# Softmax sums turned by one VectorE transposition, decay sums made by a VectorE scan, and a selector for the first units

## The chip, the cores and the metric

One core of one Trainium2 chip runs the whole program in one launch. The metric is the device time of one execution in microseconds (us), as the median of several runs. The profile comes from one further execution of the same program.

## The reference

A decay attention is followed by two feed-forward layers without biases.

```
q, k, v: (4, 8, 576, 64)   f: (4, 8, 576)
log_f  = log(clip(f, 1e-4, 1));  cum = cumsum(log_f, axis=-1)
scores = q @ k.T / 8 + cum[:, :, :, None] - cum[:, :, None, :]      (causal: -1e9 above the diagonal)
attn   = exp(scores - max); attn = attn / (sum(attn) + 1e-9); x = (attn @ v)   -> (2304, 512)
h = x @ w1_in (512 x 2048);  g = h * sigmoid(1.702 h);   y = g @ w1_out (2048 x 512)
h = y @ w2_in (512 x 2048);  g = max(h, 0) + alpha * min(h, 0);  out = g @ w2_out (2048 x 512)
```

All arrays are float32. In a row of scores the term `cum[i]` is the same for every column and drops out of the softmax; the kernel adds only `-cum[j]`.

## The kernel before, in words

A float32 product is made of three fast products: every operand is split into a rounded high part and the remainder (`hi`, `lo`), and `hi*hi + hi*lo + lo*hi` is accumulated in PSUM.

The attention works on units. A unit is a pair of heads of one batch, 16 units in all, and its 576 query rows are two chunks: rows 0 to 255 and rows 256 to 575. Batch 0 does the first chunks of its four units, then their second chunks; the other batches take a unit's two chunks one after the other. `chunk` (L869 on) makes a chunk's scores: for each tile of 128 query rows, the three split products on 64 rows of the array for each of the two heads, and a fourth product whose stationary operand is a matrix of ones and whose moving operand holds the decays `-8 cum[j]` (L884; L878 for the last 64 rows of both heads). VectorE takes the score tile out of PSUM, adds the causal mask and finds the row minimum of the negated scores (L897); ScalarE does the exponential and the row sums (L906). The four or five columns of sums in `ms` become inverses in `rc` (L920, L922, L925). Four transpositions of 32x32 blocks turn them into rows `rt` (L929), one DMA of GpSimd's queue writes the rows to a scratch in DRAM (`rscr`, L932), and two or four DMAs of that queue read them back, spread over 64 partitions, as `RR` (L935). `chunk2`, one chunk behind, transposes the exponentials on TensorE (L969), copies them to `eT` (L518 on ScalarE, L520 on VectorE), multiplies them by v (L983), and VectorE multiplies the result by `RR` into the ring `xr` (L996).

Where a first chunk of batch 0 needs keys and queries, TensorE transposes loaded tiles (`load_pe`, L770) and ScalarE and VectorE write the halves (L518, L523). Other batches are loaded in another layout and transposed by VectorE.

The decays are made at the start. `f` is loaded, clipped (L620) and its logarithm taken (L621). TensorE transposes it (L634), VectorE copies it (L639), and matmuls with a triangle of ones sum it (L648), first for columns 0 to 255, then for the other 320. ScalarE scales by -8 (L657), VectorE splits into halves (L658, L659), and DMAs write them to `cscr` in DRAM (L662, L663). The operand of the fourth product, `dk`, lies in one row for each head and half. For the first chunks of batch 0, four DMAs copy these rows out of `xr` into `w` (L1202; two of SyncE's queue, two of ScalarE's); all others are read from `cscr` into `KB` (L804).

While the attention runs, the first layer's matmuls over finished blocks of `xr` are laid between its instructions on TensorE (`gemm1`, L1027); their weights come through `wraw` (L686). After it come a tail of 768 tokens and the other products (L1050, L1271, L1453), with TensorE as good as always busy.

The order on each engine is written by a planner (`Plan.plan`), a list scheduler with a duration for each operation, and a number of buffers for each pool. Operations with a priority between 1000 and 2000, `gemm1` among them, are held back by the third number of `TRIES` when they compete with others. `Plan.run` also puts in matmuls with no use (fillers, L488) where the planner sees TensorE idle near the start. Each engine and each DMA queue runs its instructions in the order that the planner wrote, so that a waiting one holds all behind it.

Of the kernel before, what the change touches and what calls it, by code (L numbers as in the profile page):

```python
# [7 lines left out]
F32 = mybir.dt.float32  # L8
# [22 lines left out]
TRIES = [(800.0, 3000.0, 800.0)]  # L31
# [218 lines left out]
def kernel(  # L250
# [13 lines left out]
    nc = tc.nc  # L264
# [34 lines left out]
    EB, ET, QS = 2, 6, 2  # L299
# [77 lines left out]
    p_d0 = sl("w", F32R, [1, SPLIT], (1, 8192, NP))  # L377
# [14 lines left out]
    ones = att.tile([P, 2, P], F32R, name="ones")  # L392
    p_z = sb("att", "Z", 2, [P, 2, 2, 64], F32R)
# [16 lines left out]
    p_rt = sb("att", "rt", 3, [P, P])  # L410
# [204 lines left out]
    set_rows("dk0", p_d0, range(NP), lambda: part_of["w", 1][:, 2048:2048 + NP * SPLIT], NP * SPLIT, -85, (), 0, 64)  # L615
# [7 lines left out]
    plan.add([("ACT", 1300.0)], lambda e: nc.scalar.activation(warm, warm, AF.Exp), [b_f, b_id], (), -79)  # L623
    b_ch = Buf()
    chi = lambda: xr[0:BH, 3, RING - S:].bitcast(F32R)
    b_lt = Buf(ps_h)
    for part, (lo, hi) in enumerate(((0, SPLIT), (SPLIT, S))):
        ts_ = [t for t in range(NKT) if lo <= t * P < hi]
        pri = -80 if part == 0 else A0 + P1PRI

        def lf_tr(e, ts_=ts_):
            for t in ts_:
                w = min(P, S - t * P)
                nc.tensor.transpose(b_lt.ap[:w, t * BH:(t + 1) * BH], f_sb()[:, t * P:t * P + w], ident[:BH, :BH])  # L634

        def lf_cp(e, ts_=ts_):
            for t in ts_:
                w = min(P, S - t * P)
                nc.vector.tensor_copy(lfT()[:w, t], b_lt.ap[:w, t * BH:(t + 1) * BH])  # L639

        bb = Buf(ps_v)

        def cum_mm(e, lo=lo, hi=hi, bb=bb):
            tt = [t for t in range(NKT) if t * P < hi]
            for t in tt:
                w = min(P, S - t * P)
                a = max(lo, t * P)
                nc.tensor.matmul(  # L648
                    bb.ap[:BH, a - lo:hi - lo], lfT()[:w, t, :], tri()[:w, a - t * P:hi - t * P],
                    start=(t == 0), stop=(t == tt[-1]),  # L650
                )

        cs = slice(lo, hi)
        plan.add([("PE", 90.0 * len(ts_))], lf_tr, [b_f, b_id], [(b_lt, part)], pri, pad=None if part else (b_lt, lambda: b_lt.ap[:, :P], 0))
        plan.add([("DVE", 100.0 * len(ts_))], lf_cp, [(b_lt, part)], [(b_cl, part)], pri)
        plan.add([("PE", 1350.0 if part == 0 else 3300.0)], cum_mm, [(b_cl, i) for i in range(part + 1)] + [b_tri], [bb], pri, pad=(bb, lambda bb=bb: bb.ap[:, :P], 0))
        plan.add([("ACT", c_act(hi - lo, True))], lambda e, cs=cs, bb=bb, n=hi - lo: nc.scalar.mul(cums()[:, cs], bb.ap[:BH, :n], -8.0), [bb], [(b_cs, part)], pri)  # L657
        plan.add([("DVE", c_dve(hi - lo, True))], lambda e, cs=cs: nc.vector.tensor_copy(chi()[:, cs], cums()[:, cs]), [(b_cs, part)], [(b_ch, part)], pri)  # L658
        plan.add([("DVE", c_dve(hi - lo))], lambda e, cs=cs: nc.vector.tensor_tensor(  # L659
            cuml()[:, cs], cums()[:, cs], chi()[:, cs].bitcast(F32), op=ALU.subtract  # L660
        ), [(b_cs, part), (b_ch, part)], [(b_cc, part)], pri)
        plan.add(DMA(128 * (hi - lo)), lambda e, cs=cs: nc.sync.dma_start(cscr[:, 0, cs], chi()[:, cs].bitcast(F32)), [(b_ch, part)], [(b_cum, (part, 0))], A0 + P1PRI)  # L662
# [179 lines left out]
    def chunk(u, q0, q1, pri):  # L842
# [8 lines left out]
        for j, (t, a, w) in enumerate(tiles):  # L851
# [14 lines left out]
            for c0 in range(0, ext, step):  # L866
# [5 lines left out]
                def mm(e, pms=pms, a=a, w=w, c0=c0, c1=c1, f0=f0):  # L872
# [7 lines left out]
                    for i, (x, y) in enumerate(((qh, kh), (qh, kl), (ql, kh), (None, dk))):  # L880
                        for hh in range(2):
                            r = slice(64 * hh, 64 * hh + 64)
                            l = ones[r, 0, :w] if x is None else x.ap[r, a - qo:a - qo + w]
                            nc.tensor.matmul(pms[hh].ap[:, f0:f0 + c1 - c0], l, y.ap[r, c0:c1], start=i == 0, stop=i == 3, skip_group_check=True)  # L884
# [640 lines left out]
```

## Time and profile before

| | us |
|---|---|
| median of 3 runs | 962.19 (961.74 to 962.71) |
| the profiled execution, its own time | 961.95 |
| its span | 960.2 |
| TensorE busy | 942.9 (98%) |
| VectorE busy | 736.1 (77%) |
| ScalarE busy | 544.1 (57%) |
| GpSimd busy | 71.1 (7%) |

The span runs from the first to the last instruction of the program; some 1.7 us of the execution's time lie around it. PE is TensorE's matmuls, PEld its weight loads, DVE VectorE, ACT ScalarE, POOL GpSimd, SPq SyncE's queue of DMA issues. A busy share is an average over the whole span: the first 250 us hold the attention and half of the first layer, where VectorE is nearly always busy too; after that VectorE and ScalarE have room.

### The profile page before, as it was taken

The numbers are of one execution on the slowest core, as the hardware profiler recorded it, in microseconds if no ns is written. First come the engines' busy times: TensorE is split into PE (matmuls) and PEld (weight loads), VectorE is DVE, ScalarE is ACT, GpSimd is POOL, SyncE is SP. The second block draws the span as 40 slices with busy tenths as digits, with TensorE's granted clock in tenths as the row PEclk, the third lists the DMA queues.
The fourth block names the chain that finished last, engine by engine and source line by source line (L and its number), as shares of the span: only waits on it lengthen the run. The fifth ranks groups of instructions, "written<-read, shape, count | busy, mean of one in ns | idle before, by whom it ended". The sixth has DMA issues, their size and how long they took to land.

```text
span 960.2 us, 18275 instructions
## 1 busy us (share of the span) xinstructions
PE 942.9 (98%) x6499; PEld 870.4 (91%) x6499; DVE 736.1 (77%) x1760; ACT 544.1 (57%) x1197; POOL 71.1 (7%) x149
## 2 busy tenths in 40 slices
PE   8999999999999999999999999999999999999998
PEld 6788787888999999888888988999999999999998
DVE  5899998996167766736758885988568978898987
ACT  6898876676344355657767774566465623221212
POOL 2321233331020000000000000000000000000000
PEclk9999999999999999999999999999999999999999
DMA  7978777542222375548796785688729495443523
GB/s 149 184 187 225 180 135 161 114 86 73 79 72 85 106 249 182 167 156 316 276 321 220 245 270 171 222 322 280 273 90 345 156 395 170 144 151 109 154 78 100
DMA packets 183132, 177.59 MB, mean 185 GB/s; under 512 B 100736, under 2 KB 156832, under 8 KB 180736
## 3 DMA queue, kind: packets, MB, share of 16 engines
q1 hardware_dynamic: 178928, 171.61, 58.1%
q0 software_dynamic: 4096, 4.80, 2.0%
q8 instruction: 51, 0.84, 0.4%
q14 instruction: 41, 0.34, 0.1%
q10 hardware_dynamic: 16, 0.01, 0.0%
HBM read 112.43 MB, written 63.92 MB: 184 GB/s over the span
## 4 chain that ended last, share of the span: by engine, by line
PE 81%; DVE 7%; DMA 4%; issue 3%; ACT 2%; SPq 1%; POOL 1%; DVEq 0%; ACTq 0%; POOLq 0%
PE bk L1050 23%; PE bk L1271 21%; PE bk L1453 19%; PE bk L1027 11%; PE bk L983 3%; PE bk L969 2%; PE bk L884 2%; DMA KB<-cscr 1%; DMA rscr<-rt 1%; PE bk L878 1%; DVE rt L929 1%; DMA RR<-rscr 1%; DVE ec L897 1%; POOL RR L935 1%; DVE ea L897 1%
## 5 line engine op out<-in xcount | busy, mean ns | idle before, releaser
L1050 PE MATMUL bk<-x,wS 128*128 128x384 f32 x912 | 160.7, 335 | 0.9 <-DVE lx L1076 0.9
L1050 PEld LDWEIGHTS bk<-x,wS 128*128 128x128 f32 x912 | 158.1, 188 | 2.0 <-DVE lx L1076 1.8
L1027 PE MATMUL bk<-xh,w 128*128 128x320 f32 (+2 forms) x640 | 148.8, 308 | 0.1
L1271 PE MATMUL bk<-lh,w 128*128 128x512 f32 (+1 forms) x640 | 147.0, 368 | 1.3 <-ACT lh L518 1.3
L1271 PEld LDWEIGHTS bk<-lh,w 128*128 128x128 f32 x640 | 112.8, 189 | 21.6 <-ACT lh L518 1.6
L1027 PEld LDWEIGHTS bk<-xh,w 128*128 128x128 f32 x640 | 108.7, 189 | 5.0 <-issue 3.2
L1027 PE MATMUL bk<-xl,w 128*128 128x320 f32 (+2 forms) x320 | 97.2, 304 | 0.0
L523 DVE TENSOR_TENSOR ll<-lx,lh 128x512 fp32r<-128x512 f32 (+1 forms) x80 | 50.8, 635 | 45.7 <-PE bk L1271 34.7
L1271 PE MATMUL bk<-ll,w 128*128 128x512 f32 (+1 forms) x320 | 81.2, 368 | 0.0
L518 ACT CAST x<-x 128x768 fp32r<-128x768 f32 (+3 forms) x41 | 33.4, 825 | 67.4 <-PE bk L1453 55.2
L1453 PE MATMUL bk<-wS,x 128*128 128x256 f32 x567 | 70.5, 283 | 0.0
L1453 PEld LDWEIGHTS bk<-wS,x 128*128 128x128 f32 x567 | 69.1, 192 | 0.0
L1453 PE MATMUL bk<-wS,lh 128*128 128x256 f32 x378 | 68.7, 283 | 0.0
L1237 ACT ACTIVATE lx<-lx 128x512 f32<-128x512 f32 (+1 forms) x80 | 47.0, 588 | 38.0 <-DVE ll L523 31.5
L1271 PEld LDWEIGHTS bk<-ll,w 128*128 128x128 f32 x320 | 57.1, 189 | 9.7
L1027 PEld LDWEIGHTS bk<-xl,w 128*128 128x128 f32 x320 | 60.5, 189 | 0.3 <-DVE xl L523 0.2
L518 ACT CAST lh<-x 128x768 fp32r<-128x768 f32 (+3 forms) x29 | 23.2, 805 | 64.7 <-PE bk L1453 49.2
L523 DVE TENSOR_TENSOR x<-x,x 128x768 fp32r<-128x768 f32 (+3 forms) x59 | 56.0, 979 | 4.2 <-ACT x L518 3.1
L1453 PEld LDWEIGHTS bk<-wS,lh 128*128 128x128 f32 x378 | 59.0, 192 | 0.0
L518 ACT COPY lx<-bk 128x384 f32<-128x384 f32 x72 | 34.1, 478 | 39.6 <-PE bk L1050 25.3
L935 POOL DMA_DIRECT2D RR<-rscr x96 | 50.0, 533 | 53.0 <-DVE xr L996 27.9
L1453 PE MATMUL bk<-wS,ll 128*128 128x256 f32 x189 | 53.5, 283 | 0.0
(190 smaller groups left out, 1966.3 us busy)
## 6 DMA issues: line engine op xcount, KB each, us to landing
h2scr<-lx SPq DMA_DIRECT2D x96, 192.0 KB, 3.7
wraw<-in_moe_w_in_dram SPq DMA_DIRECT2D x32, 512.0 KB, 4.9
wraw<-in_moe_w_out_dram SPq DMA_DIRECT2D x32, 512.0 KB, 6.9
lx<-h1scr SPq DMA_DIRECT2D x64, 256.0 KB, 3.1
x<-h2scr SPq DMA_DIRECT2D x32, 512.0 KB, 4.2
w2scr<-wS SPq DMA_DIRECT2D x5, 1792.0 KB, 7.1
tscr<-wS SPq DMA_DIRECT2D x4, 1792.0 KB
wS<-tscr SPq DMA_DIRECT2D x4, 1792.0 KB
```

What stands on the lines that cost most here:

```text
L518: nc.scalar.copy(dst, src)
L523: E[e].tensor_tensor(dst, a, b, op=ALU.subtract)
L884: nc.tensor.matmul(pms[hh].ap[:, f0:f0 + c1 - c0], l, y.ap[r, c0:c1], start=i == 0, stop=i == 3, skip_group_check=True)
L897: plan.add([("DVE", c_dve(c1 - c0) + (69.0 if c0 else 10.0))], lambda e, pm=pm, i=i, t=t, c0=c0, c1=c1, mk=mk, m0=m0, col=col, f0=f0, firs ...
L935: plan.add(DMAR(256 * w), lambda e, x=x, w=w, hh=hh: E[e].dma_start(rr.ap[64 * hh:64 * hh + 64, x:x + w], rscr[row, 2 * x + hh * w:2 * x + ...
L969: nc.tensor.transpose(pt.ap[:, i * P:(i + 1) * P], view[j, hh](t * P, t * P + P), ident)
L983: nc.tensor.matmul(pb.ap[64 * hh:64 * hh + 64, x0:x1], vr.ap[:, t, hh], et.ap[:, c0:c0 + x1 - x0], start=t == 0 and hh not in seen, stop=t ...
L1027: nc.tensor.matmul(ph.ap[:, :n], w.ap[:, a, c, :], x[c // 2].ap[:, c % 2, :n], start=(c == 0 and j == 0), stop=(c == KT - 1 and j == 2))
L1050: nc.tensor.matmul(out.ap[:, :XH], wt(a, c), x.ap[:, b, c, :], start=(st and c == 0 and i == 0), stop=(c == 1 and i == 2), skip_group_chec ...
L1237: plan.add([("ACT", c_act(n))], lambda e: nc.scalar.activation(g.ap[:, :n], raw.ap[:, :n], AF.Gelu_apprx_sigmoid), [raw], [g], pri)
L1271: nc.tensor.matmul(py[d].ap[:, :n], w[:, a, d * P:(d + 1) * P], (lo if x else h).ap[:, :n], start=(k == 0 and (a, x) == (0, 0)), stop=(k = ...
L1453: nc.tensor.matmul(py[j].ap[:, t * HF:(t + 1) * HF], x.ap[:, q:q + P], w[:, o, a, :], start=(k == 0 and t == 0 and c == 0), stop=(k == NPA ...
```

## The change

Six things are changed together.

- The sums of the logarithms are made by VectorE's scan instruction (L634 of the new kernel), 256 columns and then 320, in place of TensorE's transpositions and triangle matmuls, the copies and ScalarE's scaling. The halves go to a tile `cc` of 128 partitions: high parts in 0 to 31, low parts in 32 to 63, and for the first 256 columns the same again in 64 to 127.
- The first chunks of batch 0 take the fourth product's moving operand straight from `cc`, and `sel`, made from the identity matrix by two VectorE instructions, picks a unit's rows in place of the ones. The four DMAs of L1202 and the tile they wrote are gone.
- The inverses: one addition, one reciprocal and one transposition of 128x32 in place of one or two additions, a reciprocal and four transpositions of 32x32. The one DMA that wrote `rt` is now four, one for each group of 32 partitions.
- `eT` has five buffers, not six; `rt` is 32 columns wide, not 128.
- ScalarE loads the table of the logarithm at the very start.
- The planner's numbers: `gemm1` is held back by 200, not 800, and several durations of small VectorE instructions are longer. So the order of all engines is another.

```
-TRIES = [(800.0, 3000.0, 800.0)]
+TRIES = [(800.0, 3000.0, 200.0)]
-    EB, ET, QS = 2, 6, 2
+    EB, ET, QS = 2, 5, 2
-    p_d0 = sl("w", F32R, [1, SPLIT], (1, 8192, NP))
+    cc = att.tile([P, S], F32R, name="cc")
+    sel = att.tile([P, NP, P], F32R, name="sel")
-    p_rt = sb("att", "rt", 3, [P, P])
+    p_rt = sb("att", "rt", 3, [P, 32])
...
+    def set_sel(e):
+        for i in range(2):
+            r = slice(64 * i, 64 * i + 64)
+            col = lambda c: ident[r, c + i:c + i + H:2].unsqueeze(2).broadcast_to([64, NP, P])
+            E[e].tensor_tensor(sel[r], col(64 * i), col(64 * i + BH), op=ALU.add)
...
-        def lf_tr(e, ts_=ts_):
...
-        def cum_mm(e, lo=lo, hi=hi, bb=bb):
...
+        plan.add([("DVE", 2.1 * (hi - lo) + 70.0)], lambda e, lo=lo, cs=cs: nc.vector.tensor_tensor_scan(
+            cums()[:, cs], f_sb()[:, cs], f_sb()[:, cs], cums()[:, lo - 1:lo] if lo else 0.0, ALU.add, ALU.bypass
+        ), [b_f, *([(b_cs, 0)] if lo else [])], [(b_cs, part)], pri)
+        plan.add([("DVE", c_dve(hi - lo, True), 0.0, True)], lambda e, cs=cs: nc.vector.tensor_scalar(chi()[:, cs], cums()[:, cs], -8.0, None, op0=ALU.mult), [(b_cs, part)], [(b_ch, part)], pri)
+        plan.add([("DVE", c_dve(hi - lo))], lambda e, cs=cs: nc.vector.scalar_tensor_tensor(
+            cuml()[:, cs], cums()[:, cs], -8.0, chi()[:, cs].bitcast(F32), op0=ALU.mult, op1=ALU.subtract
...
+        if not part:
+            plan.add([("DVE", c_dve(hi, True) + c_dve(hi), 0.0, True)], lambda e, cs=cs: [
+                nc.vector.tensor_scalar(cc[64:64 + BH, cs], cums()[:, cs], -8.0, None, op0=ALU.mult),
+                nc.vector.scalar_tensor_tensor(cc[64 + BH:P, cs], cums()[:, cs], -8.0, chi()[:, cs].bitcast(F32), op0=ALU.mult, op1=ALU.subtract),
+            ], [(b_cs, 0), (b_ch, 0)], [b_c2], pri)
...
-                            l = ones[r, 0, :w] if x is None else x.ap[r, a - qo:a - qo + w]
+                            elif u["first"]:
+                                l, m = sel[r, u["hp"], :w], cc[r, c0:c1]
...
-            for g in range(0, P, 32):
-                nc.vector.transpose(rt.ap[:32, g:g + 32], rc.ap[g:g + 32])
-        plan.add([("DVE", 4 * 85.0)], turn, [rc], [rt], pri)
-        plan.add(DMAR(nc_ * 512), lambda e: E[e].dma_start(rscr[row, :nc_ * P].rearrange("(c n) -> c n", c=nc_), rt.ap[:nc_, :]), [rt], [rs], pri, 1500.0)
+        plan.add([("DVE", 150.0, 0.0, True)], lambda e: nc.vector.tensor_scalar_add(ms.ap[:, 6:6 + nc_], ms.ap[:, 6:6 + nc_], 1e-9), (), ks, pri)
+        plan.add([("DVE", 165.0)], lambda e: nc.vector.reciprocal(rc.ap[:, :nc_], ms.ap[:, 6:6 + nc_]), [*ks, *frc], [rc], pri)
+        plan.add([("DVE", 190.0)], lambda e: nc.vector.transpose(rt.ap, rc.ap), [rc], [rt], pri)
+        rows = rscr[row, :nc_ * P].rearrange("(c g n) -> g c n", c=nc_, g=4)
+        for g in range(4):
+            plan.add(DMAR(nc_ * 128), lambda e, g=g: E[e].dma_start(rows[g], rt.ap[32 * g:32 * g + nc_, :]), [rt], [(rs, g)], pri, 1500.0)
...
-    for i, (src, bsrc) in enumerate(((chi, b_ch), (cuml, b_cc))):
-        for hh in range(2):
-            r = 64 * hh + 32 * i + 1
-            plan.add(DMA(4 * NP * SPLIT) if hh == 0 else [("ACTQ", 4 * NP * SPLIT / 360.0)], lambda e, r=r, hh=hh, src=src: E[e].dma_start(
```

TensorE, from the program's start to the first score of the first unit, before. L488 are fillers (each row is two instructions of the trace for every x), L770 transpositions of keys and queries, L634 and L648 the decays, L884 scores:

```order
L488 MATMUL bk_87<-ident 128x128 x5
L770 MATMUL bk_87<-ident,raw_122 128x128 x2
L634 MATMUL bk_88<-ident,xr 128x32 x4
L634 MATMUL bk_88<-ident,xr 64x32
L770 MATMUL bk_89<-ident,raw_130 128x128 x2
L648 MATMUL bk_90<-xr 32x256
...
L770 MATMUL bk_89<-ident,r_136 128x128 x2
L770 MATMUL bk_90<-ident,r_136 128x128 x2
L488 MATMUL bk_91<-ident 128x128 x4
L884 MATMUL bk_91<-w_100,w_169 128x128
```

Now, the same stretch (L489 fillers, L754 transpositions, L873 scores; `cc,sel` is the fourth product):

```order
L489 MATMUL bk_89<-ident 128x128 x5
L754 MATMUL bk_89<-ident,raw_126 128x128 x2
L489 MATMUL bk_90<-ident 128x128
L754 MATMUL bk_90<-ident,raw_132 128x128 x2
L489 MATMUL bk_91<-ident 128x128 x6
L754 MATMUL bk_91<-ident,r_137 128x128 x2
L489 MATMUL bk_92<-ident 128x128 x4
L873 MATMUL bk_92<-w_151,w_164 128x128
```

The decays' matmuls are gone, seven more fillers stand there, and twelve of the transpositions that stood ahead of the first score come behind it.

SyncE's queue, from the first values of `v` to the first reads of `KB`, before (L1202 the copied decay rows, L740 keys and queries of batch 0, L686 weights of the first layer, L804 the decay operand of the second chunks):

```order
L821 DMA r_163<-in_v_dram 128x2x64 x6
L1202 DMA w_100<-xr 1x4x256 x2
L662 DMA cscr<-xr 32x256
L663 DMA cscr<-xr 32x256
L740 DMA r_212<-in_k_dram 128x8x64 x2
L662 DMA cscr<-xr 32x320
L740 DMA r_212<-in_k_dram 64x8x64
...
L686 DMA wraw_388<-in_moe_w_in_dram 128x4x256
L686 DMA wraw_402<-in_moe_w_in_dram 128x4x256
L804 DMA KB_108<-cscr 4x576
L804 DMA KB_109<-cscr 4x576
```

Now (L646, L647 for `cscr`, L724 keys and queries, L805 and L809 v, L788 the decay operand, L670 weights):

```order
L805 DMA r_158<-in_v_dram 128x2x64 x6
L646 DMA cscr<-cc 32x256
L647 DMA cscr<-cc 32x256
L724 DMA r_225<-in_k_dram 128x8x64 x2
L724 DMA r_225<-in_k_dram 64x8x64
...
L809 DMA VR_102<-in_v_dram 64x2x64
L788 DMA KB_109<-cscr 4x576
L805 DMA VR_102<-in_v_dram 128x4x64 x2
L788 DMA KB_110<-cscr 4x576
...
L670 DMA wraw_406<-in_moe_w_in_dram 128x4x256
```

The two reads of `KB` stand nine and seven issues earlier and ahead of all weights; the third tile of keys no longer stands behind a write of the second part of the decays.

## Rows read from the trace of the kernel before

**Rows 1.** The page, part 1: busy time, share of the span, instructions.

```profile
PE 942.9 (98%) x6499; PEld 870.4 (91%) x6499; DVE 736.1 (77%) x1760; ACT 544.1 (57%) x1197; POOL 71.1 (7%) x149
```

**Rows 2.** Busy time by stretch: stretch, length, engines' busy us (instructions), granted clock, DMA.

```profile
14.00:30.00 16.00, 13.95 (x141) 11.58 (x140) 14.90 (x74) 11.66 (x45) 4.35 (x8) 1.00 0.85 197
30.00:32.00 2.00, 0.32 (x2) 0.32 (x4) 0.06 (x1) 0.66 (x1) 0.03 (x1) 0.94 1.06 346
32.00:34.00 2.00, 2.00 (x11) 1.16 (x9) 1.04 (x4) 0.99 (x3) 0.00 (x0) 0.50 1.38 179
34.00:36.00 2.00, 2.00 (x12) 1.84 (x12) 1.95 (x7) 1.24 (x5) 1.05 (x2) 0.70 1.24 149
48.00:216.00 168.00, 163.48 (x1448) 137.85 (x1447) 160.12 (x571) 134.10 (x392) 46.90 (x90) 1.00 0.69 155
```

**Rows 3.** Timeline of PE to the first score: start us, us, what, [idle before <-releaser].

```profile
1.47 2.50 PE L488 MATMUL bk<-ident 128*128 128x128 f32 x10 [1.47 <-POOL ident L546]
4.60 0.66 PE L770 MATMUL bk<-ident,raw 128*128 128x128 f32 x2 [0.64 <-DMA raw<-in_k_dram]
...
5.91 0.69 PE L770 MATMUL bk<-ident,raw 128*128 128x128 f32 x2
6.53 5.34 PE L648 MATMUL bk<-xr 128*32 128x256 f32 x14
11.80 1.75 PE L770 MATMUL bk<-ident,r 128*128 128x128 f32 x14
13.39 1.06 PE L488 MATMUL bk<-ident 128*128 128x128 f32 x8
14.38 0.33 PE L884 MATMUL bk<-w,w 64*128 64x128 f32 x2
```

**Rows 4.** Timeline of DVE at the start.

```profile
2.75 0.45 DVE L620 TENSOR_SCALAR xr<-xr 32x576 f32<-32x576 f32 x1 [0.62 <-DMA xr<-in_f_dram]
...
8.77 0.42 DVE L659 TENSOR_TENSOR xr<-xr 32x256 fp32r<-32x256 f32 x1
9.22 0.76 DVE L597 TENSOR_TENSOR KB<-ident 128x576 fp32r<-128x576 f32 x1
```

**Rows 5.** Timeline of ACT at the start.

```profile
4.56 0.68 ACT L621 ACTIVATE xr<-xr 32x576 f32<-32x576 f32 x1
```

**Rows 6.** Timeline of SyncE's queue, 10 to 32 us.

```profile
11.03 1.51 SPq L1202 DMA_DIRECT2D w<-xr  x2
15.60 0.70 SPq L740 DMA_DIRECT2D r<-in_k_dram  x1
...
26.41 1.11 SPq L804 DMA_DIRECT2D KB<-cscr  x2
```

**Rows 7.** Timeline of PE, 14 to 50 us: its two long waits.

```profile
20.52 0.27 PE L770 MATMUL bk<-ident,r 64*128 64x64 f32 x1 [1.60 <-DMA r<-in_k_dram]
31.68 0.64 PE L884 MATMUL bk<-KB,ones 64*128 64x384 f32 x2 [2.13 <-DMA KB<-cscr]
```

**Rows 8.** Three lines by source: engine, operation, duration ns min/median/max, first and last start.

```profile
L929 DVE STREAM_TRANSPOSE rt<-rc x128: 156/199/206, 20.0 to 246.2; 32x32 f32<-32x32 f32 x128
...
L932 POOL DMA_DIRECT2D rscr<-rt x32: 518/529/661, 21.1 to 246.7; - x32
...
DMA to landing us min/median/max: 1.5/2.2/6.5
```

**Rows 9.** One trip of the sums: timelines of POOL and of DVE.

```profile
43.51 0.53 POOL L932 DMA_DIRECT2D rscr<-rt  x1 [5.72 <-DVE rt L929]
45.72 2.06 POOL L935 DMA_DIRECT2D RR<-rscr  x4 [1.68 <-DMA rscr<-rt]
...
53.39 0.48 DVE L996 TENSOR_TENSOR xr<-bk,RR 128x320 f32<-128x320 f32 x1
```

**Rows 10.** L996 by source: its instructions, and what VectorE stood idle for there (us, times).

```profile
L996 DVE TENSOR_TENSOR xr<-bk,RR x32: 383/435/492, 36.0 to 280.8; 128x256 f32<-128x256 f32 x16, 128x320 f32<-128x320 f32 x16
...
  DMA RR<-rscr: 2.2, 2
```

More of the change, by code (lines that the diff above doesn't have):

```diff
@@ L621 @@
     plan.add([("ACT", 600.0)], lambda e: nc.scalar.activation(f_sb(), f_sb(), AF.Ln), (), [b_f], -80)
-    plan.add([("ACT", 1300.0)], lambda e: nc.scalar.activation(warm, warm, AF.Exp), [b_f, b_id], (), -79)
+    plan.add([("ACT", 1300.0)], lambda e: nc.scalar.activation(warm, warm, AF.Exp), [b_f], [b_warm], -79)
     b_ch = Buf()
-    chi = lambda: xr[0:BH, 3, RING - S:].bitcast(F32R)
-    b_lt = Buf(ps_h)
+    chi = lambda: cc[0:BH]
     for part, (lo, hi) in enumerate(((0, SPLIT), (SPLIT, S))):
-        ts_ = [t for t in range(NKT) if lo <= t * P < hi]
@@ L653 @@
-        cs = slice(lo, hi)
[L654 to L657, printed above, removed]
@@ L882, in mm @@
                             r = slice(64 * hh, 64 * hh + 64)
-                            l = ones[r, 0, :w] if x is None else x.ap[r, a - qo:a - qo + w]
-                            nc.tensor.matmul(pms[hh].ap[:, f0:f0 + c1 - c0], l, y.ap[r, c0:c1], start=i == 0, stop=i == 3, skip_group_check=True)
-                rd = [*((x, p_) for x in (kh, kl) for p_ in pr(c1)), *((dk, (i, p_)) for i in range(2) for p_ in (range(2) if u["first"] else pr(c1))), b_one, *u["fdk"]]
+                            if i < 3:
+                                l, m = x.ap[r, a - qo:a - qo + w], y.ap[r, c0:c1]
+                            elif u["first"]:
+                                l, m = sel[r, u["hp"], :w], cc[r, c0:c1]
+                            else:
+                                l, m = ones[r, 0, :w], y.ap[r, c0:c1]
+                            nc.tensor.matmul(pms[hh].ap[:, f0:f0 + c1 - c0], l, m, start=i == 0, stop=i == 3, skip_group_check=True)
+                rd = [*((x, p_) for x in (kh, kl) for p_ in pr(c1)), *([b_sel, (b_ch, 0), (b_cc, 0), b_c2] if u["first"] else ((dk, (i, p_)) for i in range(2) for p_ in pr(c1))), b_one, *u["fdk"]]
                 rd += [z] if w < P else [qh, ql]
@@ L901, in chunk @@
                     if w == P:
-                        last.append((t, i, 0, c1, col, 6 + col))
+                        last.append((t, i, 0, c1, col, 6 + 2 * i + j))
                     else:
@@ L1198 @@
     units = {no: operands(no, no) for no in range(NP)}
[L1199 to L1204 removed]
     units.update((no, operands(no, no)) for no in range(NP, 2 * NP))
     def first_weights():
[L1208 removed]
+        over = {3: p_k0.bufs[:2], 4: p_k0.bufs[2:], 6: p_q0.bufs[:2], 7: p_q0.bufs[2:], 8: p_v0.bufs, 9: p_v0.bufs, **{m: p_r0.bufs[:4] if m < 13 else p_r0.bufs[4:] for m in range(10, NM)}}
         for m in range(NM):
```

54 lines of the change are left out of this document (10 added, 44 removed).

## The prediction

> **What bounds the kernel now.** I read the page's first part, then the busy times by stretch, and then the timelines of the start. The page says TensorE is busy for 942.9 of 960.2 us [rows 1]. So the time can fall in two ways only: TensorE gets less to do, or it waits less or runs faster in the 17 us and some stretches where it doesn't run well. The stretches show where those are [rows 2]. From 48 to 216 us TensorE is idle for 168.00 - 163.48 = 4.5 us, while VectorE is busy for 160.12 of 168 (95%): two engines near their limit, TensorE a little nearer. The start is different. There the reader is to see that a busy TensorE isn't a useful one [rows 3]: up to the first score at 14.38 us it runs 18 transpositions of keys and queries, and otherwise fillers (10 at the start, 8 at the end) and the decays' matmuls, 5.34 us of them in one piece, which all else on TensorE stands behind. [...] The change touches the start, both waits, and VectorE's load in the attention. Of the stages after 250 us it changes only small choices between engines, and I carry a gain at the start through to the end in full, because TensorE is the bound from there on.
>
> **Part 1, the first score.** It is at 14.38 us. Two things decide when it comes now, VectorE's chain and TensorE's own row. VectorE's chain: the selector is two instructions of 64x512, which I price by the row of 128x576 at 0.76 us [rows 4], 0.7 each. VectorE had been idle for 0.62 us ahead of the clip, so the clip starts 0.8 us later and ends at 2.75 + 0.8 + 0.45 = 4.0. The logarithm takes 0.68 us [rows 5]; its table is already there, where it used to start at 4.56: 4.7. A scan isn't in the trace. Its lower bound is the 0.42 us of a subtraction of 32x256 [rows 4], its upper one twice that; I take 0.6, between them, for 256 columns and 0.75 for 320. [...] From 5.3 us VectorE's order has the keys' low half, the first high part, the second scan, the low part, both again for the other 64 partitions, and the queries' low half: six instructions that I price at 0.42 each and one at 0.75, 3.3 us, so 8.6. TensorE's own row: it starts on the first keys at 4.60 as before, and has to get through 6 transpositions and 22 filler instructions up to the score. [...] At the slow pace that is 5.5 us of fillers and 2 us of transpositions, 12.1; at the fast pace 2.9 + 1.4, so 8.9. I take 10.4, the middle. That is 4.0 us earlier, but 12 transpositions that used to come first now come later, 12 x 1.75/14 = 1.5 us. Gain 2.5; bounds: 14.38 - 8.9 - 1.5 = 4.0 above, and 14.38 - 12.1 - 1.5 = 0.8 below, or 0 if the next us runs at the slow pace too.
>
> **Part 2, the wait for the third tile of keys.** TensorE waits 1.60 us [rows 7] for a tile issued at 15.60 [rows 6]. In that queue it now has no copied decay rows (1.51 us) and no write of the second part ahead of it, so it goes out about 2.4 us earlier, near 13.2; TensorE comes to it 2.5 us earlier by part 1, but by the new order with the fourth unit's scores and one chunk's transposed exponentials done, which used to come after it. So the wait should mostly go. I take 1.3 of 1.60; bounds 0 and 1.6.
>
> **Part 3, VectorE in the first four chunks.** From 14 to 30 us VectorE is busy for 14.90 of 16 us and TensorE for 13.95, ten fillers among them [rows 2], so here it is VectorE that the chunks wait for. Each chunk loses three of four transpositions of 199 ns [rows 8]; the one that is left has four times the partitions and the same 32 columns, and I price it the same. Four chunks x 3 x 0.2 = 2.4 us. What is late next is ScalarE, busy for 11.66, and transfers at a DMA share of 0.85; so I count half, 1.2; bounds 0 and 2.4.
>
> **Part 4, the wait for KB.** The read is issued at 26.41 and TensorE goes on at 31.68, after 2.13 us of idle time [rows 6, 7]. Nine issues less stand ahead of it: the two copies of 1.51 us, and five reads of v and two of weights, which I price at the 0.55 us of a KB issue [rows 6], 3.9 us, and some 0.4 us between them. So it goes out near 20.6. Landing took 5.2 us with weights in the queue ahead; a small transfer of the other queue lands in 2.2 [rows 8]: 22.8 to 25.8, I take 24. TensorE asks for it at 31.68 - 2.13 = 29.55, less 2.5 + 1.3 + 1.2, at 24.5. I count 1.7 of the 2.13. The slow clock behind the wait cost 2 x 0.50 + 2 x 0.30 = 1.6 us [rows 2]; with a short wait only a little of it stays, and I count 1.4. Gain 3.1; bounds 0 (the wait only moves) and 3.7.
>
> **Part 5, the attention from 48 to 216 us.** VectorE loses 0.6 us in each of the 24 remaining chunks and an addition in half of them, some 15 us of 160. But TensorE is the fuller engine there, and all that it can win is its 4.5 us of idle time. Against it stand three prices. GpSimd's queue issues four writes for one, 24 x 3 x 0.53 = 38 us more [rows 8] of a queue that is busy for 46.90 of 168 us [rows 2]. One eT buffer is gone. And more of the first layer between the chunks (held back by 200, not 800) brings its copies out of PSUM into the time when VectorE and ScalarE are fullest. I take a gain of 1.0, nearest to the row that says there is little to win; bounds +4.5, and -6 if the new order fits worse. The `rt` buffers are smaller at no price, since three are kept.
>
> **The sum.** 2.5 + 1.3 + 1.2 + 3.1 + 1.0 = 9.1 us. Against the profiled execution's own 961.95 us (span 960.2, the rest lies around it) that is 952.85; the median of the runs shown stands 0.24 above the profiled one, and I forecast 953.0 us.
>
> **The rivals.** (a) It gets slower because the inverses come late. A trip of the sums is one write issued at 43.51, four reads issued by 47.78, and the multiplication that uses them at 53.39 [rows 9]; the last read lands 2.2 us later at the writes' pace [rows 8] and 5.2 at that of KB, so at 50.0 to 53.0, with 0.4 to 3.4 us in hand. Three more issues cost 3 x 0.53 = 1.6 us of it, and VectorE's saved 0.6 gives part back. It decides as soon as a trip is more than its reserve late, for then VectorE stands still at the multiplication, in order, with the next chunk's scores behind it, and TensorE runs out of work after that. If half of the 32 chunks lost 1 us so, 16 us would go: 953 + 16 = 969. Against it: in 32 multiplications VectorE stood still for such a read twice, 2.2 us in all [rows 10], and the new order knows that there are four writes. [...] (b) The start is bound by transfers. DMA share is 0.85 from 14 to 30 us and over 1 from 30 to 36 [rows 2]; then parts 1 to 3 only bring the waits forward, and what is left is part 4 and a little: 958.5. For it speaks the wait at 20.52, against it that the queue's issues, not the engines, order the tiles. (c) VectorE's relief is worth more: part 3 in full and all of part 5, 953.0 - 1.2 - 3.5 = 948.3; it takes a new order in which TensorE always has the first layer at hand. (d) Gains at the start and losses in the attention cancel, as 9.1 - 1.0 = 8.1 against 6 to 10: no change.
>
> **Chances.** The forecast 0.56, (a) 0.10, (b) 0.15, (c) 0.13, (d) 0.06. Faster and slower are counted from 0.2% (1.9 us), about what a measurement of this kernel can tell from no change. Of the forecast and (b) I move 0.02 to no change: faster 0.82, the same 0.08, slower 0.10. The range from 946 to 960 leaves out (a) and most of (d), and little of (c): about 0.8.
>
> **What will show it.** Part 1: the first score between 9 and 12 us, and no matmuls of the decays. Part 2: a wait under 0.5 us before the third tile of keys. Part 4: KB issued before all weights, no wait of 2 us for it, and a granted clock of 1.00 from 24 to 36 us. Part 3: one transposition of near 0.2 us for each chunk. Part 5: TensorE idle for about 3.5 us in the 168 us that now lie between 48 and 216. I am wrong if VectorE waits at the multiplication by RR for more than a few us in all, if the clock is low for long at the start, or if TensorE's idle time in the attention grows past 10 us.

## The result, and the profile after

The changed kernel takes 950.27 us (median of 4 runs, 949.17 to 951.64) against 961.97 us (4 runs, 961.13 to 962.71): a ratio of 0.988, 95% interval 0.986 to 0.989, or 11.7 us less. The forecast was 953.0, with a range of 946 to 960. The profiled execution took 950.24 us with a span of 948.5, so the spans differ by 11.7 us too, and the rows can be added up to it.

The page's first part, after; it answers to [rows 1]:

```profile
PE 935.5 (99%) x6482; PEld 869.3 (92%) x6482; DVE 719.4 (76%) x1657; ACT 539.4 (57%) x1186; POOL 120.2 (13%) x243
```

TensorE is busy for 7.4 us less (942.9 to 935.5) and idle for 4.3 us less (960.2 - 942.9 = 17.3, now 13.0). Busy time by stretch shows where; these rows answer to [rows 2]:

```profile
14.00:30.00 16.00, 15.09 (x137) 11.71 (x135) 14.11 (x64) 13.05 (x49) 10.43 (x20) 1.00 0.87 202
30.00:32.00 2.00, 2.00 (x19) 1.33 (x17) 2.00 (x7) 2.00 (x8) 0.27 (x2) 1.00 1.12 298
32.00:34.00 2.00, 2.00 (x20) 1.69 (x20) 1.84 (x10) 2.00 (x6) 0.88 (x2) 1.00 1.43 177
34.00:36.00 2.00, 1.45 (x13) 0.78 (x10) 1.58 (x5) 2.00 (x6) 0.53 (x1) 1.00 1.10 148
48.00:216.00 168.00, 164.22 (x1441) 145.01 (x1440) 130.16 (x428) 120.50 (x343) 66.75 (x128) 1.00 0.67 156
```

The hole at 30 us is closed and the granted clock stays at 1.00. VectorE's load from 48 to 216 us fell by 30 us, more than the 15 that the change takes away there, since some of its work now stands elsewhere (over the whole span it fell by 16.7). TensorE's idle time in those 168 us went from 4.5 to 3.8 us only.

TensorE up to the first score, after; it answers to [rows 3] (L489 fillers, L754 transpositions, L873 scores):

```profile
4.58 0.66 PE L754 MATMUL bk<-ident,raw 128*128 128x128 f32 x2 [0.67 <-DMA raw<-in_k_dram]
5.03 0.63 PE L489 MATMUL bk<-ident 128*128 128x128 f32 x2
5.62 0.66 PE L754 MATMUL bk<-ident,raw 128*128 128x128 f32 x2
6.07 2.76 PE L489 MATMUL bk<-ident 128*128 128x128 f32 x12
8.63 0.73 PE L754 MATMUL bk<-ident,r 128*128 128x128 f32 x2
9.15 1.71 PE L489 MATMUL bk<-ident 128*128 128x128 f32 x8
10.79 0.55 PE L873 MATMUL bk<-w,w 64*128 64x128 f32 x6
```

The first score comes at 10.79 us instead of 14.38. The 5.34 us of the decays are gone, and the reader is to see what stands in their place: fillers at 0.21 to 0.23 us each (2.76/12, 1.71/8).

VectorE at the start, after; it answers to [rows 4]:

```profile
1.99 1.47 DVE L616 TENSOR_TENSOR sel<-ident 64x512 fp32r<-64x512 f32 x2
3.49 0.50 DVE L624 TENSOR_SCALAR xr<-xr 32x576 f32<-32x576 f32 x1
4.74 0.68 DVE L634 TENSOR_TENSOR_SCAN xr<-xr 32x256 f32<-32x256 f32 x1 [0.75 <-ACT xr L625]
...
6.23 0.87 DVE L634 TENSOR_TENSOR_SCAN xr<-xr 32x320 f32<-32x320 f32 x1
...
8.32 0.42 DVE L523 TENSOR_TENSOR w<-bk,w 128x256 fp32r<-128x256 f32 x1
```

SyncE's queue and TensorE's timeline at the two waits, after; they answer to [rows 6, 7]. Both waits are small now:

```profile
20.41 0.61 SPq L788 DMA_DIRECT2D KB<-cscr  x1
```
```profile
21.98 0.27 PE L754 MATMUL bk<-ident,r 64*128 64x64 f32 x1 [0.33 <-DMA r<-in_q_dram]
```

The waits of TensorE in its first 250 us, after (line, us in total, times, longest): the one that adds up to most, none of its three over 1.0 us, and that for KB.

```profile
PE bk L950 <- ACT eT L518: 2.5, 3, 1.0
...
PE bk L873 <- DMA KB<-cscr: 0.2, 1, 0.2
```

TensorE's waits from 216 us on by what they wait for, first of before, then of after. The four of before come to 2.7 us, the one of after to 0.4:

```profile
PE bk L1271 <- ACT lh L518: 1.3, 1, 1.3
PE bk L1050 <- DVE lx L1076: 0.9, 2, 0.6
PE bk L884 <- DVE ms L897: 0.3, 1, 0.3
PE bk L878 <- DVE ms L897: 0.2, 1, 0.2
```
```profile
PE bk L1246 <- DVE ll L523: 0.4, 1, 0.4
```

The inverses by source, after; they answer to [rows 8, 10] (the third row counts what VectorE stood idle for at L977, the multiplication by RR):

```profile
L910 DVE STREAM_TRANSPOSE rt<-rc x32: 170/202/213, 16.2 to 274.6; 128x32 f32<-128x32 f32 x32
...
L913 POOL DMA_DIRECT2D rscr<-rt x128: 518/521/738, 16.7 to 276.6; - x128
...
DMA to landing us min/median/max: 1.5/2.3/6.9
```
```profile
L977 DVE TENSOR_TENSOR xr<-bk,RR x32: 384/452/492, 30.9 to 282.3; 128x256 f32<-128x256 f32 x16, 128x320 f32<-128x320 f32 x16
...
  DMA RR<-rscr: 7.8, 4
```

One transposition of four times the partitions takes 202 ns against 199. Four writes an item, all of 0.52 us, land in a median of 2.3 us, where the one landed in 2.2.

**TensorE's 7.4 us of busy time.** The groups of TensorE's instructions by line, before (busy us, mean ns):

```profile
L884 PE MATMUL bk<-KA,QA 64*128 64x384 f32 (+3 forms) x336 | 42.2, 353 | 0.7 <-ACT gg L518 0.3 <-DVE ms L897 0.3
...
L488 PE MATMUL bk<-ident 128*128 128x128 f32 x40 | 7.1, 323 | 1.5 <-POOL ident L546 1.5
L648 PE MATMUL bk<-xr 128*32 128x320 f32 (+4 forms) x14 | 5.3, 558 | 0.0
...
L634 PE MATMUL bk<-ident,xr 32*128 32x32 f32 (+1 forms) x5 | 0.7, 283 | 0.1
```

and after:

```profile
L873 PE MATMUL bk<-KA,QA 64*128 64x384 f32 (+3 forms) x336 | 40.8, 351 | 0.0
...
L489 PE MATMUL bk<-ident 128*128 128x128 f32 x42 | 9.2, 385 | 1.4 <-POOL ident L545 1.4
```

The decays' matmuls take away 5.3 + 0.7 = 6.0 us. The fillers give back 2.1, the transpositions of keys and queries 0.8, since more of both run at the slow pace ahead of 10.8 us: 32 fillers in place of 10 (0.21 to 0.25 us each in the rows of 8 to 12, against 0.13 at 13.4 before), and 6 transpositions in place of 4 (medians of 430 and 448 ns, against 273 ns from 11.8 us on). The other 4.3 us are the same matmuls in less time: 1.4 of them here, in the 336 scores. So the saving of 6.0 us of work is worth 3.1 of the 11.7, less idle time 4.3, and the same matmuls in less time 4.3. The low clock of the kernel before can be 1.7 of these at most (2 x 0.06 + 2 x 0.50 + 2 x 0.30, from [rows 2]).

### The profile page after: what moved, and what is told of

Its sections match the earlier page's. It is cut to its first block, busy times and chain, and to the rows that moved or that the text cites. A ratio compares the mean times of both kernels' runs of the same rounds, so it can differ in the third digit from the quotient of the medians.

```text
span 948.5 us, 18224 instructions
## 1 busy us (share of the span) xinstructions
PE 935.5 (99%) x6482; PEld 869.3 (92%) x6482; DVE 719.4 (76%) x1657; ACT 539.4 (57%) x1186; POOL 120.2 (13%) x243
## 4 chain that ended last, share of the span: by engine, by line
PE 85%; DVE 1%; ACT 1%; DMA 1%; issue 0%; DVEq 0%; ACTq 0%
PE bk L1031 23%; PE bk L1246 20%; PE bk L1428 19%; PE bk L1008 12%; PE bk L964 3%; PE bk L873 3%; PE bk L950 3%; PE bk L862 1%; DMA wraw<-in_moe_w_out_dram 1%; DVE w L523 0%; DVE td L1140 0%; ACT ea L895 0%; ACT ec L895 0%; DVE ll L523 0%; ACT L1212 0%
## 5 line engine op out<-in xcount | busy, mean ns | idle before, releaser
L913 POOL DMA_DIRECT2D rscr<-rt x128 | 66.6, 528 | 129.5 <-DVE rt L910 103.2
L518 ACT CAST x<-x 128x768 fp32r<-128x768 f32 (+3 forms) x41 | 33.4, 825 | 67.4 <-PE bk L1428 52.9
L1246 PEld LDWEIGHTS bk<-ll,w 128*128 128x128 f32 x320 | 56.9, 189 | 10.2 <-DVE ll L523 0.7
L518 ACT COPY lx<-bk 128x384 f32<-128x384 f32 x72 | 34.2, 479 | 38.8 <-PE bk L1031 25.1
```

Of the source, the lines that this page charges most:

```text
L518: nc.scalar.copy(dst, src)
L913: plan.add(DMAR(nc_ * 128), lambda e, g=g: E[e].dma_start(rows[g], rt.ap[32 * g:32 * g + nc_, :]), [rt], [(rs, g)], pri, 1500.0)
L1246: nc.tensor.matmul(py[d].ap[:, :n], w[:, a, d * P:(d + 1) * P], (lo if x else h).ap[:, :n], start=(k == 0 and (a, x) == (0, 0)), stop=(k = ...
```

## The experiments

To say where in the program a kernel is ahead, I counted TensorE's matmuls in order of start, without fillers and without those of the decays, each weighed with its columns at full speed, and took the time at which the same amount is done in two profiled executions. The difference is called the lead. Within the attention it is rough, since orders differ; past 375 us, where all attention is done, it is not. The changed kernel's lead is 2.1 us when the kernel before is at 25.1 us, 3.0 at 29.0, 6.8 at 35.3 (past the wait for KB), 7.3 at 40.0, 5.1 at 98.6 and 10.1 at 375.8, and 12.0 at TensorE's last matmul. How rough it is shows when a transposition is weighed once to four times its columns: at 25.1, 35.3, 98.6 and 375.8 the lead stays as it is, at 29.0 it lies between 2.9 and 4.3, at 40.0 between 6.2 and 7.3.

**Three parts alone (e1, e2, e3).** In the kernel before, the new inverses alone, the new number of the order alone, and both:

```diff
-            for g in range(0, P, 32):
-                nc.vector.transpose(rt.ap[:32, g:g + 32], rc.ap[g:g + 32])
+        plan.add([("DVE", 190.0)], lambda e: nc.vector.transpose(rt.ap, rc.ap), [rc], [rt], pri)
...
+        for g in range(4):
+            plan.add(DMAR(nc_ * 128), lambda e, g=g: E[e].dma_start(rows[g], rt.ap[32 * g:32 * g + nc_, :]), [rt], [(rs, g)], pri, 1500.0)
```
```diff
-TRIES = [(800.0, 3000.0, 800.0)]
+TRIES = [(800.0, 3000.0, 200.0)]
```

> The kernel before with the new inverses alone: one transposition of 128x32 and four writes of 128-byte rows, the planner's number still 800, six eT tiles, decays as before. Theory S (most of the 11.7 us comes from the start: first score, the two waits for transfers, the slow clock): 960 to 961.5 us, since the wait for KB stays and only a little is won in the attention. Rival V (VectorE's 21 us less work is what counts): under 957. Rival P (the trip of the sums with three more issues costs time by itself): over 963.

> The kernel before with the planner's number 200 alone: more of the first layer's matmuls stand between the chunks. Theory S: 960.5 to 963, as VectorE is still 95% busy in the attention and the start is the same. Rival O (the order is what counts, the other parts are decoration): 953 to 957. Rival V: 962 or slower, since the copies of the first layer's results meet a full VectorE.

> The kernel before with the new inverses and the number 200, decays as before: all of the change but the start and the sixth eT tile. Theory S: 956.5 to 959, the 3 to 5 us that the attention gives. Rival V or O: 951 to 954. If the start gives everything: 961 to 962. The wait of 2.1 us for KB and the granted clock of 0.5 behind it should still be there.

Measured against 960.89 us of before: inverses 959.77 (ratio 0.999, 0.997 to 1.001), order 957.72 (0.997, 0.995 to 0.998), both 957.94 (0.997, 0.996 to 0.998). The inverses alone can't be told from nothing, though VectorE is busy for 18 us less in the whole span; the order is worth 3.2 us; the two together are worth no more than the order. Theory S is right for the inverses (0.2 us off) and for both together; the order alone lies between S and rival O. All three keep the wait for KB and the slow clock behind it, 0.50 from 34 to 36 us in each, as this row of the inverses alone shows:

```profile
34.00:36.00 2.00, 2.00 (x12) 1.72 (x12) 1.55 (x7) 1.93 (x8) 0.41 (x2) 0.50 1.25 145
```

**The changed kernel without the new order (e4).** The same diff of TRIES the other way round, in the changed kernel.

> The changed kernel with the planner's number back at 800: the start and the inverses of the change, the first layer's matmuls held back as before. Theory S: 952 to 955, the start's 7 us and a little of the attention. Rival O: 958 or more. If the order is worth nothing: 950.

Measured: 958.68 us (0.998, 0.996 to 0.999), rival O: 2.2 us less than before, where the changed kernel is 11.7 less. Its lead is 6.8 us at 35.3 and 7.2 at 40.0, just as in the changed kernel; it is 0.9 at 98.6 and 2.7 at 375.8. The waits of TensorE in its first 250 us (before: 2.1, 1.6, 1.5, 1.3; changed kernel: none over 1.0 but the first) and three stretches behind them:

```profile
PE bk L950 <- ACT ed L895: 1.9, 1, 1.9
PE bk L964 <- DVE xr L977: 1.7, 1, 1.7
...
PE bk L873 <- DMA KB<-cscr: 1.3, 1, 1.3
```
```profile
42.00:48.00 6.00, 5.97 (x43) 4.58 (x44) 4.41 (x13) 3.62 (x10) 2.09 (x4) 0.72 1.04 279
76.00:80.00 4.00, 4.00 (x44) 3.60 (x46) 4.00 (x13) 2.68 (x7) 2.07 (x4) 1.00 0.27 65
112.00:120.00 8.00, 6.38 (x37) 5.35 (x37) 5.89 (x19) 8.00 (x27) 4.16 (x9) 0.79 0.37 76
```

So the start's gain can be lost again in the attention. Two of these waits are paid twice, as idle time and as a clock of less than 1.00 behind them: the 1.3 us at 40.7 (0.72 from 42 to 48) and the 1.9 us at 110.5 (0.79 from 112 to 120). Not every longer wait is: behind the 1.7 us at 74.2 the clock stays at 1.00, as it does in the kernel before behind the 1.60 us at 18.9 [rows 2, 7].

**What the slow clock behind the wait for KB costs (e5).** In the kernel before, ten fillers ahead of the product that waits; nothing else moves.

```diff
-pad=(pms[0], lambda x=pms[0], f0=f0, n=min(P, c1 - c0): x.ap[:, f0:f0 + n], 4 if pri == A0 and j == 0 else 0))
+pad=(pms[0], lambda x=pms[0], f0=f0, n=min(P, c1 - c0): x.ap[:, f0:f0 + n], 4 if pri == A0 and j == 0 else 10 if pri == A0 + NP and j == 0 else 0))
```

> The kernel before with ten filler matmuls (20 in the trace, some 2.2 us) ahead of the scores that wait for KB, and all else in the same order on every engine. The wait itself stays. Theory C (a part of the 11.7 us is the slow clock that a wait of 2 us leaves behind): the granted clock is 1.00 from 32 to 36 us, the work after it is done some 1.6 us earlier, and the time falls to 959 to 960.5 if the attention lets it through, or stays at 961 if the next wait eats it. Rival (the clock falls for another reason): the granted clock still falls to 0.5 near 34 us.

Measured: 959.32 against 960.34 us (0.9985, 0.9975 to 0.9996). The clock, 0.94, 0.50 and 0.70 in [rows 2], is 1.00 throughout:

```profile
30.00:32.00 2.00, 1.95 (x18) 1.51 (x16) 0.00 (x0) 0.68 (x1) 0.00 (x0) 1.00 1.01 335
32.00:34.00 2.00, 1.99 (x15) 1.53 (x16) 1.51 (x5) 0.85 (x3) 1.05 (x2) 1.00 1.41 193
34.00:36.00 2.00, 2.00 (x19) 1.44 (x20) 2.00 (x9) 2.00 (x7) 0.00 (x0) 1.00 1.25 154
```

The lead is 1.2 us at 35.3 and still 1.1 at 375.8. The order of all useful work is the same, so the clock is shown as the cause of 1.0 to 1.2 us (the interval alone allows 0.4 to 2.4).

**Each small write twice (e6), a miss.**

```diff
-E[e].dma_start(rows[g], rt.ap[32 * g:32 * g + nc_, :])
+[E[e].dma_start(rows[g], rt.ap[32 * g:32 * g + nc_, :]) for _ in range(2)]
```

> The changed kernel with each of the four writes of the inverses issued twice, so eight issues of 0.52 us for a chunk, the order of all else the same. Theory S (the trip has a reserve of 1 to 3 us in most chunks): 2.1 us more in each trip brings waits at the multiplication by RR and 951 to 956. Rival (the trip has much in hand): 950. Rival P (the trip was at its limit with four writes): over 965, for 32 times 2.1 us are 67.

Measured: 1182.17 us (1.231, 1.229 to 1.234). It did not test what it was for. The second write goes where the first went, so it waits for the first to land: GpSimd's queue stood still for it 128 times, 242.8 us in all, and each trip grew by landings and not by issues. It does show that late inverses stop TensorE: it is busy for 109 of 168 us from 48 to 216, at a clock of 0.79.

**Each small write a second time, elsewhere (e9).** The scratch gets 32 more rows, which nobody reads; so a trip grows only by four issues.

```diff
+        copy_ = rscr[BH + row, :nc_ * P].rearrange("(c g n) -> g c n", c=nc_, g=4)
-E[e].dma_start(rows[g], rt.ap[32 * g:32 * g + nc_, :])
+[E[e].dma_start(rows[g], rt.ap[32 * g:32 * g + nc_, :]), E[e].dma_start(copy_[g], rt.ap[32 * g:32 * g + nc_, :])]
```

> The changed kernel, with each of the four small writes issued twice, the second time into scratch rows of its own that nobody reads; so each trip of the sums only has four more issues of about 0.53 us ahead of its reads, 2.1 us, with no write that waits for an earlier one. Theory (the trip's reserve is more than 2 us, rival a was never near): 950 to 953 us, first-layer multiplications of VectorE (line of xr, RR) wait for RR under 20 us in all. Rival (the reserve is nearly used up, the changed kernel stands at its edge): 960 us or more, with VectorE standing still at the multiplication 1 us or more in many of the 32, and TensorE behind it.

Measured: 979.52 us, the rival: slower than the kernel before (1.020, 1.017 to 1.022), and some 30 us over the changed kernel. The page of the profiled execution, the longest of the five with 983.44 us, and the multiplication by RR by source:

```profile
PE 948.9 (97%) x6482; PEld 876.5 (89%) x6482; DVE 718.5 (73%) x1657; ACT 539.6 (55%) x1186; POOL 186.1 (19%) x371
```
```profile
L978 DVE TENSOR_TENSOR xr<-bk,RR x32: 381/452/492, 34.2 to 316.5; 128x256 f32<-128x256 f32 x16, 128x320 f32<-128x320 f32 x16
its engine sat idle before it (us, times) until:
  DMA RR<-rscr: 40.4, 15
```

GpSimd's queue isn't full (it issues for 89 of the 168 us from 48 to 216, and for 67 in the changed kernel), and the landings are as before (2.3 us). What counts is the length of one trip: 2.1 us more, which the order was not written for, make VectorE wait at 15 of 32 multiplications, and TensorE loses 18.8 us by waiting (980.7 - 948.9 = 31.8 us idle, 13.0 in the changed kernel) and 13.4 by running slower (mean clock 0.989). My theory here, that there are over 2 us in hand, is wrong.

**Fewer fillers ahead of the first score (e7), and another number (e8).** Both in the changed kernel.

```diff
-pad=(pms[0], lambda x=pms[0], f0=f0, n=min(P, c1 - c0): x.ap[:, f0:f0 + n], 4 if pri == A0 and j == 0 else 0))
+pad=(pms[0], lambda x=pms[0], f0=f0, n=min(P, c1 - c0): x.ap[:, f0:f0 + n], 0))
```
```diff
-TRIES = [(800.0, 3000.0, 200.0)]
+TRIES = [(800.0, 3000.0, 400.0)]
```

> The changed kernel without the four filler rows (8 in the trace, 1.7 us) that stand ahead of the first score, all else in the same order. Theory (TensorE's own row, not VectorE's chain, sets the first score): the first score comes at 9.2 to 9.6 us, not 10.79, and the time falls by up to 1 us, 949 to 950.3. Rival (the fillers bring the clock up): the scores run at the slow pace and the time is 950 to 951.5.

> The changed kernel with the planner's number at 400, between 200 and 800 (958.68 in the run before). Theory O (holding back the first layer's matmuls leaves TensorE without work, and the more the longer): 950.5 to 955. Rival (each order has its own accidents): it may lie anywhere from 949 to 960, and its waits stand at other places than with 800.

Measured: 951.28 us (0.991, 0.989 to 0.993) and 950.84 (0.990, 0.988 to 0.992), both within 1.1 us of the changed kernel's 950.27, which was not run again beside them. So e7 misses its theory's time. Without the fillers the first score comes 1.4 us earlier, so TensorE's own row set it:

```profile
9.37 0.90 PE L873 MATMUL bk<-w,w 64*128 64x128 f32 x6
```

But the lead is the same by 25 us (2.2 against 2.1). The first six scores take 0.90 us in place of 0.55, as the rival said, and TensorE then waits 0.86 and 0.43 us for tiles of queries from 20.3 us on, where the changed kernel waits 0.33. An earlier first score is worth nothing by itself here: the transfers take it back. And 400 does what 200 does; with 800 the gain is lost.

**One eT tile less, without and with the old inverses (e10, e11).**

```diff
-    EB, ET, QS = 2, 5, 2
+    EB, ET, QS = 2, 4, 2
```

> The changed kernel with four eT tiles instead of five. It is the base for the next run, which needs the room. Theory (the eT buffers are not what bounds it): 950 to 952.5 us. Rival (each buffer counts, the fifth already cost something): 954 us or more, with TensorE's transpositions and VectorE's copies waiting for eT.

> Four eT tiles, the new start and the new order (200), but the inverses as before (four VectorE transpositions and one write a chunk). Beside the run with four eT tiles it tells what the inverses are worth inside the whole. Theory (gains are not additive: the start wins some 7 us by 40 us and the order keeps them; the inverses give little where TensorE has work at hand): 953 to 955 us, 2 to 4 us over the run with four eT tiles, VectorE busy some 148 of 168 us from 48 to 216. Rival (VectorE's relief is what keeps the start's gain): 957 us or more, 6 us over it or more, with the longest waits of TensorE for VectorE's eT, xr and lh.

Five of the changed kernel become four; e11 also puts the inverses of e1 back to those of before. Measured: 953.64 us (0.992, 0.990 to 0.994), and with the old inverses 959.82 (0.999, 0.997 to 1.001). So in this setting the inverses are worth 6.2 us, as the rival said, where alone they were worth 1.1. But the longest waits of e11 are not those that the rival named: 1.4 us for the minima `ms` at 38.7 and 1.9 for ScalarE's `u2t` at 395. The first is between its theory and its rival: TensorE waits for eT only 0.2 us in the first 262 us, but the new order has other waits, and a clock of 0.89 from 14 to 30 and of 0.86 from 36 to 48 us. The lead of e11 is 5.6 us at 40.0, 0.4 at 98.6 and 3.1 at 375.8. The row from 36 to 48 us, of e10 and of e11; the changed kernel has 11.04 us busy there, at 1.00:

```profile
36.00:48.00 12.00, 9.32 (x65) 7.52 (x65) 11.42 (x30) 10.01 (x28) 5.01 (x10) 0.86 0.84 192
```
```profile
36.00:48.00 12.00, 9.84 (x68) 7.84 (x68) 11.00 (x33) 10.83 (x29) 3.61 (x7) 0.86 0.87 169
```

**An early KB in the kernel before (e12).** The second part of the decays is summed with the first, still by TensorE, and the order is that of 200.

```diff
-        pri = -80 if part == 0 else A0 + P1PRI
+        pri = -80
```

> The kernel before with the new order (200) and the second part of its decays, still summed by TensorE, put with the first, so that KB is issued early; fillers, selector and inverses as before. Theory (of the start it is the wait for KB and the slow clock behind it that cost, 3 to 4 us): 953.5 to 956 us, no wait for KB over 0.5 us, clock 1.00 from 24 to 36 us, first score near 15.5. Rival (the whole start must be shorter; an early second part only delays the first scores): 957 to 960 us, as with the order alone.

Measured: 960.03 us (0.999, 0.998 to 1.001): the rival's time, but not for its reason. The wait for KB is gone and the clock is 1.00 from 24 to 36 us, the first score comes at 13.39, 1.0 us earlier than before, and the lead is 3.9 us at 35.3. At 52.9 it is -1.7: TensorE waits 1.3 us for `ms` at 39.0 and 2.5 for eT at 48.6, and at 98.3 another 2.7 for `xr`. The stretch from 80 to 130 us:

```profile
80.00:130.00 50.00, 45.04 (x362) 38.66 (x362) 45.85 (x148) 37.54 (x96) 11.36 (x22) 0.93 0.77 171
```

## Why the prediction was right, and where it was not

**Part 1.** The mechanism holds for the first score, but little of its gain lasts. The first score came at 10.79 us (10.4 forecast), and TensorE's row sets it, not VectorE's chain, which had the queries' low half ready at 8.74 (8.6 forecast). The two paces of the forecast are those of the fillers in [rows 3], 2.50/10 = 0.25 us each at 1.5 us and 1.06/8 = 0.13 at 13.4; they ran at the slow one, 0.21 to 0.25, not at the middle. The scans took 0.68 and 0.87 us, where I had 0.6 and 0.75. Those two were my estimate between the 0.42 us of a subtraction of 32x256 and twice that; no run shows the factor of two, and the scan of 256 columns took 1.6 times the 0.42. The 0.2 us more changed nothing: VectorE's chain was ready at 8.74, and TensorE's row came to the score at 10.79. The score comes 3.6 us earlier, and 1.5 go to the twelve transpositions behind it, as forecast. But the sum has no term for what else stands there now: ten fillers where before there were four (0.71 and 0.83 us against 0.71), and a wait of 0.46 us for the exponentials at 14.7. The lead is 0.5 to 0.8 us when the kernel before comes to its wait for the third tile at 18.9, and 2.1 at 25.1, where parts 1 and 2 were to bring 3.8. So part 1 is the term that was sized too large: 2.5 forecast, under 1 measured, near its lower bound of 0.8. (The upper bound takes 1.4 us for six transpositions at the fast pace, where its own 1.75/14 each makes 0.75; nothing rests on it.)

**Parts 2 and 3.** The wait for a third tile went from 1.60 to 0.33 us, as forecast, though it is now one for queries. VectorE's load from 14 to 30 us fell by 0.8 us only: the transpositions fell from 3.2 to 0.8, but 2.5 us of the second chunks' score tiles now stand in the stretch. The prediction counts ten fillers of the kernel before in these 16 us; there are sixteen, and ten of them stand in one piece ahead of the wait for KB:

```profile
26.29 1.38 PE L488 MATMUL bk<-ident 128*128 128x128 f32 x10
```

The new order has none there, a gain of 1.2 us that no part of the sum names. Parts 1 to 3 were to bring 5.0 us by the time of the wait for KB; the lead there is 3.0 (2.9 to 4.3).

**Part 4.** KB was issued at 20.41 (20.6 forecast), and its wait is 0.2 us (0.4 forecast). The lead grows by 3.8 us over it by the rough value at 29.0 (3.1 forecast), of which e5 shows 1.0 to 1.2 for the clock, where I had counted 1.4. From 25.1 to 35.3, where the lead is firm, it grows by 4.7, and parts 3 and 4 had 4.3: the 2.1 us of the wait, the 1.2 of the fillers, and the clock.

**Part 5.** TensorE's idle time from 48 to 216 us is 3.8 us, where I had said about 3.5. But the attention was worth more than my 1.0: from 35.3 to 375.8 us the lead grows by 3.3, and from there by 1.9. It doesn't grow evenly. Up to 98.6 it falls by 1.7, as TensorE idles for 3.4 us in that work where it idled for 1.0 before; behind that it grows by 5.0. The step that failed is the one that nothing changes after 250 us: TensorE's idle time from 216 us on fell by 2.2 us (0.7 to 0 up to 320, 1.3 to 0.4 up to 520, 5.0 to 4.4 behind that), mostly in the waits for lh and lx, whose place in the order is new. Not all of it is the change's: e5 has the order of the kernel before and waits 0.2 us for lx, not 0.9, so some 0.7 us belong to the one profiled execution of before.

**The sum.** The same work of TensorE in both profiled executions, cut where the lead is firm (us; useless work is the time of the fillers and, before, of the decays, each up to the next matmul; the forecast is that of the parts that lie in the stretch):

| before, from to | idle, before and after | useless work, before and after | gain | forecast |
|---|---|---|---|---|
| 0 to 25.1 | 3.7, 3.0 | 10.2, 8.5 | 2.1 | 3.8 |
| 25.1 to 35.3 | 2.1, 0.0 | 1.2, 0.0 | 4.7 | 4.3 |
| 35.3 to 98.6 | 1.0, 3.4 | 0.7, 0.0 | -1.7 | 1.0 up to 375.8 |
| 98.6 to 375.8 | 4.2, 1.9 | 0.0, 0.0 | 5.0 | |
| 375.8 to the last matmul | 2.2, 0.4 | 0.0, 0.0 | 1.9 | 0.0 |

What a gain has beyond idle time and useless work is the same matmuls in less time: 1.7 us at most for the clock in the second row, and in the fourth row 2.7 us whose cause is not shown. 9.1 us were forecast and 11.7 measured (12.0 to the last matmul): 1.7 too much for parts 1 and 2, 0.4 too little for parts 3 and 4, and 4.2 too little for the rest. That the total is only 2.6 off is in part luck, since the errors go both ways. The experiments show a second fault, which the total hides: I carried the start's gain through in full because TensorE is the bound behind it. That is no law. Start and inverses are worth 2.2 us in e4, which lacks the order, and start and order (with four eT tiles) 1.3 in e11, which lacks the inverses. With all parts it is 11.7, with one eT tile less 7.5. So the order adds 3.2 us to the kernel before (e2), 1.8 to the inverses (e3 against e1) and 9.5 to start and inverses: what a part is worth depends on the others. The start alone has no run; what it is worth by itself stays open.

**The rivals.** (b), a start bound by transfers, did not happen: of both waits 0.3 and 0.2 us are left. But it is near, for in e7, where the start is 1.4 us shorter still, the wait for queries grows to 0.86 and 0.43 us. (d) did not happen, but e4 and e11 are what it described. (c), VectorE's relief worth more, is half right: the time lies between the forecast and its 948.3, and e11 against e10 gives the inverses 6.2 us. (a) did not happen. The changed kernel's multiplications wait 7.8 us in all, more than the few that were to show it, but 6.3 of that once at the very end, where no wait of TensorE answers to it. But e9 shows that it was near: my 0.4 to 3.4 us in hand fit the 15 late trips of 32 that an unplanned 2.1 us more makes, and this alone turns the change into a loss. The smaller rows of the writes are not what brings it near: rows of 128 bytes land in a median of 2.3 us, rows of 512 in 2.2.

**What stays open.** All variants but e5, e6, e7 and e9 have their own order, written anew, with its own small waits, some with a stretch of low clock behind them (0.72 from 42 to 48 us in e4, 0.86 from 36 to 48 in e10 and e11). That at 98.6 us a lead of 5.1 stands with all parts, and of 0.9 or 0.4 without one of them (e4, e11), is measured; why just this order has no wait over 1.0 us from the first score to 250 us is not shown. Nor is it shown which of the new order's moves takes away the waits after 216 us. No version ran that beats the changed kernel.

## What to carry to other kernels

An engine that is busy for 98% of the time does not keep a gain by itself (6.8 us at 35.3 became 2.2 at the end in e4): look whether it will have other work at hand at every later wait, and look at the clock behind each longer wait too, for some of them are paid a second time there (1.0 to 1.2 us behind the wait of 2.1, by e5). Price the parts of a change together where the order is written anew from them, for parts tried alone can show 1 and 3 us of a whole that is worth 12. Before lengthening a trip through memory, take its slack from the place where its result is used, not from how busy its queue is (in e9 it issued for 89 of 168 us, and the gain became a loss).

## What the hardware showed

- The fillers at the start ran at 0.21 to 0.25 us each, in rows of 8 to 12, up to 10.8 us, and at 0.13 us in the kernel before at 13.4. The granted clock prints as 1.00 in all of this stretch, but that isn't a measurement: the trace's records of it begin at 10.51 us in the changed kernel and at 11.29 in the kernel before, and a stretch without records prints as 1.00. Ahead of the first record a filler took 1.6 to 1.9 times the later 0.13 us; what slowed it is not shown.
- A VectorE transposition of 128x32 takes as long as one of 32x32 (202 and 199 ns), so three of four are saved in full.
- The scan takes 0.68 us for 256 columns and 0.87 for 320. The 64 columns cost it 0.19 us; the ordinary instructions that make the low parts (L638) take 0.41 and 0.48 us for the same sizes, so 0.07 for the 64.
